# Attention and spectral mixing on one core: turned tokens copied once out of PSUM and split in SBUF, other buffer counts, and a new written order

## The chip, the cores and the metric

The kernel runs on 1 core of one Trainium2 chip. The metric is device time of one execution in microseconds (us). Three executions of the kernel before took 480.16, 479.12 and 478.96 us; their median is 479.12 us. For this kernel a difference of about 0.3% (1.4 us) can be told from none.

## What is computed

```
# attention, per batch (4) and head (8), 768 tokens, head size 64
k_sum = max of k over blocks of 32;  v_sum = mean of v over blocks of 32
scores = [ scale*q@k.T inside a window of 16, scale*q@k_sum.T + log(32) ]
x = softmax(scores) @ [v, v_sum]                 # (4, 768, 512) with heads side by side
# mixing
theta = x @ w_theta
zr, zi = x*cos(theta), x*sin(theta)
y = w_tok_r @ zr + w_tok_i @ zi                  # over the 768 tokens of a batch
u = x + y
out = u + relu(u @ w_ch)
```

Products that need full fp32 accuracy are made of three passes: each operand is split into a high part, rounded to the matrix unit's fp32r, and a low part, the rest; high times high, high times low and low times high are added up in PSUM.

## The kernel before, in words

The four batches have 768 tokens each, which are six tiles of 128 tokens. The page of the profile names engines PE (TensorE), DVE (VectorE), ACT (ScalarE), POOL (GpSimd) and SP (the queue that issues the DMAs).

**Weights.** `w_theta`, `w_tok_r` and `w_tok_i` arrive as 64-bit floats, and `load_f64` (L1341) turns each block into fp32r parts by seven instructions: an absolute value (L1353), a clip (L1357), a shift (L1358), two bitwise joins (L1360, L1362), a cast to the high part (`hi_op`, L1313) and a subtraction for the low part (`lo_op`, L1319). There are four blocks `wth` of 512 columns and twelve blocks `wt` of 768 columns. All of them are made while the first batch is under way. The working tile `f` has two buffers, and the block sums of later batches' values (L1399) load into the same two.

**Per batch.** `prepass` loads the keys (`kn`, two halves of heads) and takes block maxima on DVE (L1382). Three buffers hold `kn`, so one half of the next batch's keys can arrive early. For the first batch the scores read `kn` directly; for later ones POOL or ACT copy the window out of `kn` into a tile `k` with one buffer (L1313, `k<-kn`).

**Per tile of tokens.** `att_tile` makes the scores (L1447); `att_half`, twice, does the masked minimum on DVE (L1460), the exponential on ACT (L1464), the transpose (L1467), a copy `pt`, the product with the values (L1473) and the normalising into `xn` (L1484 or L1486), of which there are two buffers. `turn_tile` (L1490) transposes `xn` into the PSUM bank `t` (L1495), and takes three things out of that bank: `xh` (cast, L1499), `xl` (bank minus `xh`, on DVE, L1500) and `x` (copy, L1501). `theta_tile` (L1513) makes theta in the same bank `t` by twelve matmuls (L1519), and then the angle in `w` (one buffer): L1527 on ACT, L1529 on POOL or DVE, L1530 on DVE, an absolute value (L1535 or L1537) and the two sines (L1541, L1542). Exponential and sine need different tables on ACT, so a change from one to the other costs an ACT_TABLE_LOAD. The two products with `xn` follow (L1550), the first into `w` itself, the second into `zb`; `split_z` makes `zh` and `zl` of each.

**Mixing.** `mix_step` (L1557) adds one tile of 128 tokens into the sums `m` of half the channels. It consists of four groups of six matmuls (L1571), two groups for `wtr` and two for `wti`. A batch has two halves of channels with six steps each. Below, "mixing step 1" is the step with the second tile of the batch.

**End.** After the last attention tile its pools give way to others; `u` goes to memory and back, and `out_unit` (L1602) does the last product (L1618) in eight units, two per batch.

**Order.** Nothing is scheduled automatically. The code above only records operations with what they depend on; the table ORDER (L51 to L1213) says one after another which recorded operation is issued to which engine (V is DVE, A is ACT, G is POOL, P is PE, S is SP), as a step forward or back in the list of operations. Each engine runs its own instructions strictly in that order. Operations such as a cast or a subtraction can stand on either of two engines, and the table decides which.

Of the kernel before, what the change touches and what calls it, by code (L numbers as in the profile page):

```python
# [105 lines left out]
V+12,-11,+1,+183,-125,+124,-123
S+102,-82
A+94,-3
P-159
S+202  # L110
A-42,-118,+111
S-93
P+103,+40
A-202,+172
V-221,+50,+41,+6
A-46,+171,-121
V+154
P-75
A+44,-12
S+85  # L120
A-114,-2
P+32
S-81,+214
A-123,+36,-161
V+4,+1,+151,-150
P+121
V-43,-77,+163,-1
A-53,-108,+120
S+23,+273
P-338  # L130
V+69,-1
P-67,+1
A+72
V-43
A+57
V-3
A+4,-17
V+10,-50
P-29,+40
G+307,-435  # L140
A+158
V-150
A+2,+79
V-71,+72
A+39
V+1
G-111,-8
V+80
A+80,+1
V-41,-111  # L150
P+141
A+1
P+39
V-189,+9
P+154,-43,+31
A-71,+1
V-80,+189,-188
A+121,-2
V-39,+40
G+310  # L160
P-308
G+309
A-430,+191,-110
V+123,-16,-39
P-27,+1,+1
V+65,+12,-11
G-189
V+149,+52
S-192,+16
V+177,-196  # L170
A+4
S+174
A-177
V+72,-68,+70,+69
A+56,-14,-1,-31
V-152,+4
P+149
V+1
A+31,+14,-83,-106
V+145  # L180
G-38
P+69
S-11
P+51
A-39,+10
G-186
S+14
A+171
V-78
A+1  # L190
V+37,-151,+7
A+108
V-114,+7,+217
P-73,+31
V+1
S+36,-1
P-24
A-193
V+114
A+37,+43  # L200
V-11,-68
G-114
V+219,-36,+50,-12,+15
A-84,-37
S-82,+8,+223
A-41,+14
P+76,+1
V-80
P+82
V-165  # L210
P+43
V-188,+189,+25,+172,-157
P-82,+1
G-38
P+39,+1
A-146,-3
V+189
A+28,+2,-1,-28
G-186
V+1  # L220
P+255
A-110
P+70
V-219,+5
G+145
V+110,+1,+2
A-253,+221,+1
S+25,+1
V-107,+111
A-42,+47,-37  # L230
G-219
A+141
P+155
V-295,-6,+7
P+177
A+1,-184,+258,+1
S+115
A-228
V+229
P-149  # L240
S-216,+379,+56
V-178,-82
G-184,+395,-1
V-384
P+292,-1,+3
V-298
P+207
V-67
P+157
V-35  # L250
A-83
V-38
A+79
V+41
A-53,+42,-108,+122
V-1,-54
P-29
V+30
A+177
P-206  # L260
A-180
P+181
G-177
# [1453 lines left out]
```

## Time and profile before

| | |
|---|---|
| median of the runs | 479.12 us (478.96 to 480.16) |
| the profiled execution's own time | 478.45 us |
| its span from first to last instruction | 476.6 us |
| granted TensorE clock over the span | 0.989 |
| busy PE, DVE, ACT, POOL | 446.1, 317.7, 273.7, 101.1 us |
| bytes moved | 62.12 MB, 130 GB/s in the mean |

The rows are read like this. A group's row has line, engine, operation, tile written and tiles read, partitions x elements, the count, and after the bar the busy time, the mean duration of one in ns, and the idle time of the engine just before. A row of a stretch has the stretch in us from the span's start, its length, then the busy time with the number of instructions of PE, of the weight loads (PEld), of DVE, ACT and POOL, then the granted clock, the share of the DMA engines and GB/s. A row of waits has the waiting engine and line, whom it waited for, and total, number and longest in us. A row of the timeline has start, duration, engine, line and operation, and in brackets the idle time before it with what ended it. Tiles and steps are counted here from 0 in each batch.

### The profile page before, as it was taken

The page shows a single profiled execution, that of the slowest core. Times are in us where ns is not written, and L with a number is a line of the kernel's source. Part 1 is how long each engine was busy: PE and PEld are TensorE (multiplying, and loading weights), DVE is VectorE, ACT ScalarE, POOL GpSimd, SP SyncE. Part 2 cuts the span into 40 slices and gives each one's busy share as a digit, 9 for nine tenths or more (in the row PEclk, how much of TensorE's full clock was granted, in tenths as well). Part 3 has the DMA queues.
Part 4 walks back from the last instruction along what each step waited for, and adds up shares of the span by engine and source line. Part 5 has one row for each costly group of instructions (what it writes and reads, how often), then busy time and mean ns, then how long its engine had stood idle before and what let it go on. Part 6 is the DMA issues. An engine that isn't in the chain of part 4 may idle for free.

```text
span 476.6 us, 10041 instructions
## 1 busy us (share of the span) xinstructions
PE 446.1 (94%) x3864; PEld 380.7 (80%) x3864; DVE 317.7 (67%) x905; ACT 273.7 (57%) x582; POOL 101.1 (21%) x124
## 2 busy tenths in 40 slices
PE   0875979999999999999999999999999999999997
PEld 0354867788888888888888888888888889999996
DVE  4989999997574985559556676475655694333343
ACT  2679999878456898956575676656853310001110
POOL 1224244341120021003212110212100413131310
PEclk9988899999999999999999999999999999999999
DMA  8999552065411515024314201110301540724763
GB/s 311 369 342 336 174 191 80 0 233 160 162 57 35 179 65 151 22 77 139 126 52 151 82 30 35 57 41 0 85 1 45 187 145 33 239 99 152 246 209 116
DMA packets 30767, 62.12 MB, mean 130 GB/s; under 512 B 3584, under 2 KB 14080, under 8 KB 30720
## 3 DMA queue, kind: packets, MB, share of 16 engines
q1 hardware_dynamic: 30720, 61.49, 39.2%
q8 instruction: 30, 0.49, 0.4%
q14 instruction: 17, 0.14, 0.1%
HBM read 48.90 MB, written 12.58 MB: 129 GB/s over the span
## 4 chain that ended last, share of the span: by engine, by line
PE 78%; DVE 8%; DMA 6%; issue 3%; ACT 2%; POOL 1%; SPq 0%; ACTq 0%; POOLq 0%; DVEq 0%
PE m L1571 38%; PE c L1618 14%; PE t L1519 12%; PE av L1473 5%; PE p L1467 4%; PE s L1447 3%; DMA wt<-wti 2%; PE t L1495 2%; DMA x<-vn 2%; DMA f<-vT 2%; DVE f L1360 1%; DVE f L1362 1%; DMA kn<-kT 1%; POOL wt L1319 1%; DVE e L1460 1%
## 5 line engine op out<-in xcount | busy, mean ns | idle before, releaser
L1571 PE MATMUL m<-wt,zh 128*128 128x512 f32 (+1 forms) x768 | 170.2, 343 | 0.0
L1571 PEld LDWEIGHTS m<-wt,zh 128*128 128x128 f32 x768 | 119.0, 188 | 16.1 <-issue 0.6
L1571 PE MATMUL m<-wt,zl 128*128 128x512 f32 (+1 forms) x384 | 98.8, 338 | 0.0
L1464 ACT ACTIVATE e<-e,st 128x118 f32<-128x118 f32 x192 | 66.0, 388 | 22.3 <-DVE st L1460 21.5
L1519 PE MATMUL t<-wth,xh 128*128 128x512 f32 x192 | 62.8, 409 | 6.6 <-DVE xl L1500 6.6
L1618 PE MATMUL c<-cuh,wth 128*128 128x384 f32 x256 | 65.6, 337 | 0.0
L1571 PEld LDWEIGHTS m<-wt,zl 128*128 128x128 f32 x384 | 58.7, 188 | 8.5
L1460 DVE CUSTOM_DVE_ANT_0 e<-s,cs 128x118 f32<-128x118 f32 x192 | 46.6, 272 | 8.4 <-PE p L1467 6.2
L1519 PEld LDWEIGHTS t<-wth,xh 128*128 128x128 f32 x192 | 35.0, 194 | 15.1 <-DVE xl L1500 6.0
L1618 PEld LDWEIGHTS c<-cuh,wth 128*128 128x128 f32 x256 | 45.9, 188 | 0.5
L1313 ACT CAST cuh<-cu 128x384 fp32r<-128x384 f32 x20 | 9.6, 511 | 63.9 <-DMA cu<-u_scratch 61.6
L1618 PE MATMUL c<-cul,wth 128*128 128x384 f32 x128 | 43.3, 338 | 0.0
L1623 DVE SCALAR_TENSOR_TENSOR cu<-c,cu 128x384 f32<-128x384 f32 x32 | 17.2, 554 | 39.1 <-PE c L1618 34.9
L1519 PE MATMUL t<-wth,xl 128*128 128x512 f32 x96 | 38.6, 402 | 0.0
L1473 PEld LDWEIGHTS av<-v,pt 118*64 118x64 f32 x768 | 26.8, 138 | 14.6 <-issue 7.7
L1473 PE MATMUL av<-v,pt 118*64 118x65 f32 x768 | 33.3, 229 | 3.0 <-DVE xn L1486 2.6
L1467 PE MATMUL p<-cs,e 128*118 128x128 f32 x192 | 31.1, 285 | 1.6 <-ACT e L1464 0.8
L1529 POOL TENSOR_SCALAR w<-w 128x512 f32<-128x512 f32 x16 | 10.4, 647 | 98.5 <-ACT w L1527 87.5
L1550 DVE TENSOR_TENSOR w<-xn,w 128x512 f32<-128x512 f32 x24 | 17.1, 712 | 18.5 <-ACT w L1542 18.5
L1527 ACT ACTIVATE w<-t,bmagic 128x512 f32<-128x512 f32 x24 | 16.4, 684 | 20.6 <-PE t L1519 14.0
L1319 POOL TENSOR_TENSOR zl<-w,zh 128x512 fp32r<-128x512 f32 x9 | 12.7, 1413 | 72.5 <-DVE zh L1313 39.5
L1319 POOL TENSOR_TENSOR cul<-cu,cuh 128x384 fp32r<-128x384 f32 x17 | 17.0, 1012 | 52.0 <-ACT cuh L1313 32.3
(86 smaller groups left out, 714.5 us busy)
## 6 DMA issues: line engine op xcount, KB each, us to landing
v<-vg SPq DMA_DIRECT2D x48, 195.0 KB, 3.1
q<-qg SPq DMA_DIRECT2D x24, 256.0 KB, 4.9
cu<-u_scratch SPq DMA_DIRECT2D x32, 192.0 KB, 3.2
out<-cu SPq DMA_DIRECT2D x32, 192.0 KB, 2.0
kn<-kT SPq DMA_DIRECT2D x6, 798.0 KB, 7.1
wt<-wtr SPq DMA_DIRECT2D x6, 768.0 KB, 9.4
wt<-wti SPq DMA_DIRECT2D x6, 768.0 KB, 8.7
f<-vT SPq DMA_DIRECT2D x12, 384.0 KB, 4.0
```

Source lines behind the costliest of these rows:

```text
L1319: op(f"VG tt {n}", lambda e: V[e].tensor_tensor(dst(), src(), hi().bitcast(F32), op=ALU.subtract), reads, writes)
L1447: mm("s" if len(parts) == 1 else "s0", [lambda p=p, g=g, h=h, c=c, kk=kk: nc.tensor.matmul(sc[h].get()[ROW[g], p, c], q.get()[ROW[h], p, R ...
L1460: op("V ttr", lambda eng, n=n: nc.vector.tensor_tensor_reduce(e.get()[:, n], sc[n % 2].get()[:, 2 * a + n // 2], mask(m), -SCALE, 3.0e38, ...
L1464: op("A exp", lambda eng, n=n: nc.scalar.activation(e.get()[:, n], e.get()[:, n], AF.Exp, bias=st.get()[:, n:n + 1], scale=-1.0), [(st, n) ...
L1467: mm("tr", [lambda n=n: nc.tensor.transpose(tp.get()[:NK, n], e.get()[:, n], ident()) for n in range(NH)], [e, (cs, "ident")], [tp])
L1473: mm("av", [lambda n=n, g=g: nc.tensor.matmul(xa.get()[ROW[g], n], t.get()[:, n, ROW[g]], v[g].get()[:NK, NH * a + n], start=True, stop=Tr ...
L1519: calls = [lambda t=t, xx=xx, k=k, c=c: nc.tensor.matmul(th.get(), xx.get()[:, c], w_th[c].get()[:, k], start=(c == 0 and t == 0), stop=(c ...
L1527: op(f"A psumb {DM}", lambda e: nc.scalar.activation(r(), th.get(), AF.Identity, bias=bmagic.get(), scale=1.0 / TWO_PI), [th, bmagic], [R])
L1550: op(f"V tt {DM}", lambda e, z=z, hc=hc: nc.vector.tensor_tensor(z(), xn[b, i].get().rearrange("p h d -> p (h d)")[:, None, hc].broadcast_ ...
L1571: nc.tensor.matmul(acc[th], zz.get()[:, r, cc], w_t[s, r].get()[:, k, TT[th]], start=(s == r == t == 0 and (th == 0 or c == 0)), stop=(s = ...
L1618: calls = [lambda t=t, k=k, uu=uu, c=c, co=co, acc=acc: nc.tensor.matmul(acc.get(), w_ch[c].get()[:, k, co * P:(co + 1) * P], uu.get()[:, ...
L1623: op(f"V ttp {HT}", lambda e, co=co, acc=acc: nc.vector.scalar_tensor_tensor(u.get()[:, co], acc.get(), 0.0, u.get()[:, co], ALU.max, ALU. ...
```

## The change

Three things are edited. First, `turn_tile`: the bank `t` is read once, into `x`; `xh` is cast from `x`, and `xl` is `x` minus `xh`, both in SBUF, and the subtraction may now stand on POOL too. Second, buffers: `kn` has two instead of three, `w` two instead of one, `xn` three instead of two. Third, the whole table ORDER is another one. Further code for a variant with split weights is added under `LAG`, which is 0, so it does nothing: the mixing, its weights and its matmuls stay as they were.

```diff
 ORDER = """
-S+64
-A+1
...
+S+80
+V+1,+1,+1,+1,-79,-2
...
-TUNE = dict(XT=1, XB=2, WB=1, TB=1, XNB=2, XHB=2, FB=2, FC=2, QB=2, VB=4, KN=3, ZB=4, ZS=6, EB=2, RING=0, PC=4)
+TUNE = dict(XT=1, XB=2, TB=1, XHB=2, FB=2, FC=2, QB=2, VB=4, ZB=4, EB=2, RING=0, PC=4, WB=2, XNB=3, KN=2, ZS=6, LAG=0, XE=1)
...
-        hi_op(x_h.get, tx.get, DM, [tx], [x_h], psum=True)
-        op(f"V ttp {DM}", lambda e: nc.vector.tensor_tensor(x_l.get(), tx.get(), x_h.get().bitcast(F32), op=ALU.subtract), [tx, x_h], [x_l])
-        hi_op(lambda: x.get()[:, :, i * P:(i + 1) * P], tx.get, DM, [tx], [(x, i)], psum=True)
+        if K["XE"]:
+            here = lambda: x.get()[:, :, i * P:(i + 1) * P]
+            hi_op(here, tx.get, DM, [tx], [(x, i)], psum=True)
+            hi_op(x_h.get, here, DM, [(x, i)], [x_h])
+            lo_op(x_l.get, here, x_h.get, DM, [(x, i), x_h], [x_l])
...
         for r in range(2):
             for c in range(2):
-                mm("m", [lambda r=r, c=c: part(r, c)],
+                    mm("m", [lambda r=r, c=c: part(r, c, (0, 1), z_h, z_l)],
```

The first place is PE in the first batch, around the theta of tile 3 (`t<-wth` is theta, `m<-wt` is mixing; the numbers tell blocks of weights apart). Before, a group of mixing step 1 ends right ahead of that theta:

```order
L1571 MATMUL m_759<-wt_580,zh 128x512
L1571 MATMUL m_760<-wt_580,zh 128x256
L1571 MATMUL m_759<-wt_580,zl 128x512
L1571 MATMUL m_760<-wt_580,zl 128x256
L1519 MATMUL t<-wth_115,xh 128x512 x2
L1519 MATMUL t<-wth_115,xl 128x512
```

In the changed kernel a group of step 0 (`wt_416`) ends there, and the groups of step 1 (`wt_405`) begin behind the theta:

```order
L1626 MATMUL m_858<-wt_416,zl 128x512
L1626 MATMUL m_732<-wt_416,zl 128x256
L1571 MATMUL t<-wth_99,xh 128x512 x2
L1571 MATMUL t<-wth_99,xl 128x512
...
L1571 MATMUL t<-wth_94,xh 128x512 x2
L1571 MATMUL t<-wth_94,xl 128x512
L1626 MATMUL m_858<-wt_405,zh 128x512
L1626 MATMUL m_732<-wt_405,zh 128x256
```

Four groups of mixing (24 matmuls) that stood ahead of this theta now stand behind it.

The second place is DVE around `xl` of tile 5, the last tile of the first batch (`f<-wt` is the making of a block of weights, `e,st<-s` the masked minimum). Before:

```order
L1486 TENSOR_TENSOR xn<-av,st 128x256
L1362 SCALAR_TENSOR_TENSOR f<-wt_753,f 128x768
L1313 CAST wt_1206<-f 128x768
L1313 CAST xh<-t 128x512
L1313 COPY x<-t 128x4x128
L1500 TENSOR_TENSOR xl<-t,xh 128x512
L1399 TENSOR_REDUCE vt<-f 128x24
```

After:

```order
L1506 ISA e,st<-s_1066,cs 128x118
L1506 ISA st 128x1
L1408 SCALAR_TENSOR_TENSOR f<-wt_1001,f 128x768
L1365 TENSOR_TENSOR xl<-x,xh 128x512
L1404 TENSOR_SCALAR f<-f 128x768
L1406 SCALAR_TENSOR_TENSOR f<-wt_297,f 128x768
```

The cast and the copy out of PSUM have left DVE's queue, and the last block of weights (`wt_297`, which was `wt_753`), whose joins stood ahead of this `xl`, now stands behind it.

The third place is SP, where the keys of the second batch are issued (`kn` keys, `wt` weights, `q` queries, `v` values). Before, the first half goes out among the early weights:

```order
L1310 DMA q<-qg 128x512
L1310 DMA v<-vg 96x520
L1310 DMA kn<-kT 128x2x798
L1310 DMA wt_605<-wti 128x1536
L1310 DMA wt_607<-wti 128x1536
L1310 DMA v<-vg 96x520 x2
```

After, both halves go out together, behind the eleventh of the twelve blocks:

```order
L1356 DMA wt_842<-wtr 128x1536
L1356 DMA v<-vg 96x520 x2
L1356 DMA kn<-kT 128x2x798
L1356 DMA q<-qg 128x512
L1356 DMA kn<-kT 128x2x798
L1356 DMA q<-qg 128x512
L1356 DMA v<-vg 96x520 x2
L1356 DMA wt_1001<-wtr 128x1536
```

With two buffers both halves wait until the first batch's last scores (tile 5) have read the buffers; the twelfth block of weights stands behind them in the queue.

More of the change, by code (lines that the diff above doesn't have):

```diff
@@ L106 @@
[L106 to L263, printed above, removed]
@@ L1206 @@
-S+1
-P-15,+1
-V+1
-S+1
-P+3,+1
+S+80
+V+1,+1,+1,+1,-79,-2
+S+53
+A+1
+V+1,+1,+1,+1,+24
+S-21
+A+22
+G+1
+A-22,-3
+S-50,-4
+V+1
+S+13,-16
+V+7,-6
+G+14
+S-11
+V+1
+S+77
+G-22
+P-39
+V+36
+A+26
+S-89,+14
+V+53,+1,+1
+S-68
+V+89
+A-20
+V-41
+A+4
+V+11
+A+4
+P-33
+S+1,-14,+70
+P-55
+S+1
+V+13,-3
+A+4
+S+169
+P-182
+S+4,+81
+V-62
+A-7
+V+10,-2
+G+28
+A+2
+G+1
+S-49
+A+24,-3
+S+50
+V-5,+1,+1,-63
+A+64,-60
+P+2
+A+11
+V+28
+A-55
+V+56,+1,+18
+P+111
+A-169
+G-11
+P+24
+V+55
+S+147,-48
+V+4,+1,-2
+S-5
+A-124,-54
@@ new lines @@
+P+14
+A+1
+S+137,-64
+V+110,-1
+A-170
+V+173,-14
+A+4,-9,+8
+V+10
+A+3,-14,+13
+G-119
+V-66,+1
+G+38
+V+18
+G+1
+V+9
+P-55
+V+1,+1,+1
+P+200
+A-44,+16,+1
+P-44
+V-85,+9
+A+95
+P+12
+V-115
+A+116,-31,+1
+P+31
+V-108,-8
+A+9
+V+77,-76
+P+118
+A-11,-116
+G+1
+V+155,-2
+A-26,-117
+V+144
+P-69
+A+73
+V-42,+40
+S-139
+V-116
+A+256
+V+11
+P-82,+1,+1
+A+84,-55,-99,+141
+V+10,-2,+3
+A-81
+G+1
+P+38
+A+32,+13
+S+74,-49
+P+3
+S-50,-1
+V-139,+1,+1,+1
+A+1,+156,+3
+V-45,+1
+S-97
+V+58
+P+70
+G-142
+V+112
+P+1
@@ new lines @@
+A+224
+S+163
+V-199
+S-175
+A+239,-63
+V+73
+A+4
+V-41,+1,-225,+7
+P+292,-73
+A+42,-41
+P+28
+A+1
+V-255
+A+227
+V-220
+A-6
+V+227
+A-40
+V-47
+P+159
+V-298,+6
+P+260,-12
+A+1
+P+135
+A+52,-432
+V+177
+A+2
+V+78
+P-40
+V+29,+1,+134
+P-163,+1
+G+214
+P-213
+A+1
+G-220,+221
+V-220
+P+283,-27,+29
+V-28
+P+31
+V+107,-15
+A+49,-434,+388,+49
+G-436
+V+385,-123
+A+127,-379
+G+1
+V+214,+38,+123
+A+17
+P-139
+A+1,+125
+V-385,+177
+A+84
+V+132
+A+4
+P-111
+V+109,-3
+A-171
+V-220,+261,-255,+1
+A+388,-13,-381
@@ new lines @@
+V+173
+A+224
+V-390,-6
+A+219
+P+67,-1,+2
+A-280
+V+213,-212
+P+375,-123,+1,+1,+1
+A+1
+S+211,-116
+P+70
+A-207
+P+66
+A+96
+V-119
+S+100,-10
+G-132
+V+208,-165
+A+1,+211
+V-118
+A-92
+V+1
+A+210,-208
+V+85
+P+41
+V+35
+S-79,+4
+G-85
+P+17,+1
+V+154
+G+37
+A-176
+V+141
+P-155,+1
+V+14,+141
+A-136
+V+119
+A+50
+P-187,+1
+V+60
+P-59
+A+139
+V-76
+P+3
+V-64
+P-1
+A+66,+86
+G-82
+A+58
+V+9,+12
+P+37
+A-114,+68,+14
+P-65
+V-62,-24,+4,-2,+85
+A+65,-53,+39
+P-130
+V+115,-35,+1
+P+11
+A+133,-97
+P+3,-130,+1
@@ new lines @@
+A+4
+V-1,-173
+A+47,+44
+G-43
+V+1
+A+1
+P-188,+277
+V+48
+P-321
+V+320,-2
+A-133
+P+76
+V+1
+P-36
+V+1,+1,+35,+1
+P-262
+V+5
+P-8,+2
+A+310,+11
+V-317,+4
+A+438
+S-20
+A+21,-2
+G-217
+P+1
+V-227
+P+228,+1,+1
+G+216
+V-21,-2
+A-192
+G+1
+V+84
+P+118,-88
+A-75
+P+76
+S-344,+291,+1
+A+27,+113
+G+7
+P-170
+V+30,+1
+A+4,+13,-14,+15
+P+126,-138
+A+1
+P+39,-1
+A+93
+P-118,+28
+V-118,-50,+90,-39
+A+1
+V+39,+1
+S-312,+475
+A-253
+P+126
+V+139
+P-174
+V+189
+G-279
+V+277
+A-151
+V+136,+1
+P-96,-3
+A+103,-176,+1
@@ new lines @@
+S+25
+V-29
+P+5
+G-4
+P+16,-216,+224,+1,-8
+V+9,-219
+P+211,+1
+V+1
+P-10,+1,-6,+1
+S+25
+V+1
+A-3
+P-17,-5
+V+23,-22
+S-200,+229,-10
+V+11
+A-3
+S-26
+P+4
+G+26,-6
+V-19
+P-210,+2,+234
+S-25,-245,+251
+V-208,-2
+S+1
+P+229,+17,+1
+V-250,+227
+P+6,+18,-14,+1,+1,+13
+S-251,+260
+V+1
+P-22
+S+15,+3,+6
+V-8
+G+1
+A+2
+G+1,+3
+A+2
+G+1
+P-32,+9
+S-238
+V+230,+18
+P-9
+V-3
+P+4
+S+9
+P-8
+V+1
+P+26
+S-31
+P+37
+S-43
+P+38,+11,-10,+11
+S-38,+43
+P-24,+1,+1,+1,+10
+V+12
+P-11,+1,-6,+11
+V-4,-6
+S+17
+V+1,-24
```

1850 lines of the change are left out of this document (864 added, 986 removed).

## The prediction

> **What bounds the kernel now.** I read the busy line and the slices of the page first.
>
> ```profile
> PE 446.1 (94%) x3864; PEld 380.7 (80%) x3864; DVE 317.7 (67%) x905; ACT 273.7 (57%) x582; POOL 101.1 (21%) x124
> PE   0875979999999999999999999999999999999997
> DVE  4989999997574985559556676475655694333343
> ```
>
> A digit stands for 11.9 us. PE is full from the eleventh slice on; in the first nine it is not, and there DVE is. So I cut the span into stretches at the places where PE starts a theta (columns: PE, weight loads, DVE, ACT, POOL).
>
> ```profile
> 47.30:61.50 14.20, 13.20 (x154) 10.48 (x154) 13.62 (x50) 14.14 (x26) 5.54 (x5) 0.84 0.53 183
> 61.50:75.00 13.50, 12.05 (x134) 9.63 (x134) 13.50 (x29) 13.04 (x29) 6.61 (x8) 1.00 0.55 191
> 75.00:88.20 13.20, 11.33 (x114) 9.05 (x113) 13.06 (x32) 12.99 (x25) 3.60 (x3) 1.00 0.06 16
> 88.20:98.70 10.50, 10.20 (x93) 8.26 (x93) 10.40 (x29) 9.26 (x20) 4.46 (x4) 1.00 0.13 39
> 98.70:108.20 9.50, 9.07 (x77) 7.39 (x77) 8.61 (x26) 6.10 (x11) 3.09 (x6) 1.00 0.83 275
> ```
>
> ```profile
> 120.00:200.00 80.00, 79.77 (x766) 66.99 (x766) 53.25 (x170) 58.33 (x133) 11.66 (x22) 1.00 0.32 100
> ```
>
> From 120 to 200 us PE idles 0.23 us in 80, and its slices stay full behind that: whatever the change does for the other engines there, PE's own work is the same and nothing is to be won. Between 47.3 and 88.2 DVE is busy for 40.18 of 40.9 us and ACT for 40.17, while PE idles 4.3. What PE waits for (stretch 12 to 110 us) is one thing above all:
>
> ```profile
> PE t L1519 <- DVE xl L1500: 6.6, 5, 4.2
> ```
>
> Theta waits for `xl`. Time that PE loses there it never gets back, since it is full afterwards. The time of the kernel is PE's work plus PE's lost time in the first 108 us, and the change can only alter the second, or add losses later. The two last waits for `xl` are those of tiles 4 and 5:
>
> ```profile
> 88.20 0.70 PE L1519 MATMUL t<-wth,xh 128*128 128x512 f32 x2 [0.98 <-DVE xl L1500]
> 98.67 0.70 PE L1519 MATMUL t<-wth,xh 128*128 128x512 f32 x2 [0.17 <-DVE xl L1500]
> ```
>
> **The change, term by term.** The method: count in the two orders what DVE has ahead of these two `xl`, and what PE has ahead of these two thetas. If DVE's part shrinks by more than PE's, PE loses less. The prices:
>
> ```profile
> L1360 DVE SCALAR_TENSOR_TENSOR f<-wt,f 128x768 int32<-128x768 int32 x12 | 13.0, 1087 | 0.1
> L1362 DVE SCALAR_TENSOR_TENSOR f<-wt,f 128x768 uint32<-128x768 uint32 x12 | 12.6, 1049 | 0.0
> L1529 DVE TENSOR_SCALAR w<-w 128x512 f32<-128x512 f32 x8 | 3.9, 486 | 7.1 <-ACT w L1527 7.1
> L1550 DVE TENSOR_TENSOR w<-xn,w 128x512 f32<-128x512 f32 x24 | 17.1, 712 | 18.5 <-ACT w L1542 18.5
> L1313 DVE CAST xh<-t 128x512 fp32r<-128x512 f32 x12 | 8.2, 687 | 3.6 <-PE t L1495 3.6
> L1313 DVE CAST zh<-w 128x512 fp32r<-128x512 f32 x14 | 7.0, 501 | 1.5 <-PE m L1571 1.3
> L1500 DVE TENSOR_TENSOR xl<-t,xh 128x512 fp32r<-128x512 f32 x24 | 16.4, 683 | 2.5 <-ACT xh L1313 2.3
> L1319 DVE TENSOR_TENSOR zl<-zb,zh 128x512 fp32r<-128x512 f32 x14 | 10.7, 766 | 0.1
> L1319 POOL TENSOR_TENSOR zl<-w,zh 128x512 fp32r<-128x512 f32 x9 | 12.7, 1413 | 72.5 <-DVE zh L1313 39.5 <-ACT e L1464 17.4 <-ACT zh L1313 9.3
> L1358 DVE TENSOR_SCALAR f<-f 128x768 int32<-128x768 int32 x12 | 6.7, 562 | 0.0
> L1460 DVE CUSTOM_DVE_ANT_0 e<-s,cs 128x118 f32<-128x118 f32 x192 | 46.6, 272 | 8.4 <-PE p L1467 6.2 <-PE s L1447 1.7 <-issue 0.5
> L1313 DVE COPY pt<-p 118x512 f32<-118x512 f32 x14 | 9.6, 682 | 4.3 <-PE av L1473 3.5 <-PE p L1467 0.8
> L1319 DVE TENSOR_TENSOR wt<-f,wt 128x768 fp32r<-128x768 f32 x5 | 4.8, 957 | 0.0
> ```
>
> An `xl` out of SBUF is not in this trace. Its nearest row is the same subtraction for `zl`, 0.766 us; its ends are the 0.683 of now and the 1.413 of POOL. I take 0.766, since all six of the first batch stand on DVE in the new order. A cast of `x` to `xh` in SBUF is nearest to the cast of `zh`, 0.501.
>
> Tile 4, changed kernel minus before: two bitwise joins fewer (1.087 + 1.049 = 2.14), two L1529 moved to POOL (0.97), one product L1550 later (0.71), three masked minima later (0.82), a shift later (0.56), one copy out of PSUM gone and one cast in SBUF come (0.19): 5.39 us less. Five short ones, on weights and on sums, go three one way and two the other, and I put them at nothing. Five `xl` at 0.083 more each give 0.42 back, so 4.97 us less. PE has four mixing groups fewer ahead of this theta, by the second row here of the chain of waits:
>
> ```profile
> 145.31 0.97 PE s L1447 x32
> ...
> 148.34 1.06 PE m L1571 x6
> ```
>
> That is 4.24 us less to do, so of DVE's 4.97 us only 0.7 reach PE as less loss.
>
> Tile 5: two joins (2.14), two L1529 (0.97), a product (0.71), two shifts or clips (1.12), and three PSUM copies for one SBUF cast (2.06 - 0.50 = 1.56) fewer; one `pt` copy (0.68) and one low part of weights (0.96) more; the short ones again nothing; six `xl` 0.50 more. Together 6.50 - 2.14 = 4.36 us less. PE has one mixing group and one tile of scores less ahead of it, 2.03 us. So 2.3 us reach PE.
>
> Losses add up and never shrink. The first gate alone leaves the lost time 0.7 us lower; the idle time after it (0.30 and 0.43 us in the last two stretches to 108.2) can vanish, so at least 0.7 and about 1.4 us is won by that count, 2.3 by the second. I take the middle of 1.4 and 2.3, **1.9 us**. Ahead of tile 5's `xl` POOL also has two low parts of `wt` fewer than before; what one of those costs DVE is seen below, up to 1.5 us, so a further 0.3 us is put down for the pair, few of which coincide. The sum is 2.2 us.
>
> What I put at nothing: fewer ACT_TABLE_LOADs (36 for 42) and the work that moves between ACT, DVE and POOL after 120 us, because PE's full stretches cover it; if that cover had holes, it would show as idle PE there. The third `xn` and the earlier free bank `t` likewise: PE's transposes waited little for them. The twelfth block of weights is issued behind both key loads, which wait for tile 5's scores; mixing step 5, at the end of the batch, is the only one to use it, and DVE's joins for it stand between the `xl` of tiles 4 and 5. If the load came later than that, DVE and tile 5's `xl` would be held as long as it is late; I put it at nothing.
>
> At the end unit 6 of the last product needs the last mixing step's sums by way of memory (L1587, store, load, split).
>
> ```profile
> 439.53 33.82 PE c L1618 x192
> ```
>
> ```profile
> cu<-u_scratch SPq DMA_DIRECT2D x32, 192.0 KB, 3.2
> ...
> u_scratch<-x SPq DMA_DIRECT2D x16, 256.0 KB, 3.3
> ```
>
> The 192 matmuls are units 4 to 7, 8.5 us each. Before, units 4 and 5 stood between, 16.9 us; in the new order mostly unit 5, 8.5 us, against 6.5 us of DMA with an addition and a split around it. It is just covered, as I count, since unit 6 begins with channels that are there earlier: nothing, at worst 1 us.
>
> The profiled execution took 478.45 us, 0.67 under the median. 478.45 - 2.2 = 476.25, and with the 0.67 the forecast for the median is **476.9 us** (own range 475.4 to 478.2, from gains of 0.9 to 3.7: the lower with `xl` at 1.413 for part of the tiles, the upper with all of POOL's relief).
>
> **A rule against the change.** The new subtraction reads two tiles in SBUF where the old one read one and PSUM. Two pairs of rows, first POOL and then DVE:
>
> ```profile
> 83.54 1.82 POOL L1319 TENSOR_TENSOR wt<-f,wt 128x768 fp32r<-128x768 f32 x1 [0.57 <-ACT wt L1313]
> 96.81 1.85 POOL L1319 TENSOR_TENSOR wt<-f,wt 128x768 fp32r<-128x768 f32 x1 [1.62 <-DVE wt L1313]
> ```
>
> ```profile
> 83.72 2.46 DVE L1360 SCALAR_TENSOR_TENSOR f<-wt,f 128x768 int32<-128x768 int32 x1
> ```
>
> ```profile
> 97.84 0.68 DVE L1500 TENSOR_TENSOR xl<-t,xh 128x512 fp32r<-128x512 f32 x1
> ```
>
> The join with two SBUF operands that started inside POOL's subtraction took 2.46 us against the 1.049 that its twin L1362 takes in the mean, and ended after POOL had; the `xl` out of PSUM that ran inside another took its usual 0.68. So an `xl` out of SBUF can now lose up to 1.5 us to POOL. The Trainium skill, "SBUF — State Buffer", section "Who interferes with whom", says so as a rule: a DVE instruction with two SBUF inputs and a GpSimd instruction that reads SBUF exclude each other, and the second to start waits. These rows agree; by the rule the time is that of the first rival below, without it that of the forecast.
>
> **The rivals.**
> *Nothing is won (25%).* By the mechanism just shown: POOL is busy for 23.3 of the 60.9 us in the first five stretches, so of six `xl` two or three meet it, at 0.8 us in the mean, 2.0 us on DVE, against which the gain of 2.2 is gone. 478.45 - 0.2 + 0.67 = 478.9 us. Against it: much of POOL's time is in instructions of other kinds.
>
> *More is won (17%).* An early hole closes: theta of tile 1 waited longest, and after it the same twelve matmuls were slower.
>
> ```profile
> 47.28 1.22 PE L1519 MATMUL t<-wth,xh 128*128 128x512 f32 x2 [4.18 <-DVE xl L1500]
> ```
>
> ```profile
> 47.28 4.70 PE t L1519 x11
> ...
> 126.30 2.77 PE t L1519 x12
> ```
>
> 4.18 + (4.70 - 2.77) = 6.1 us lie there. With two `w`, tile 1's angle need not wait for tile 0's split, and the engines' queues may flow better: two thirds of it, 4.0 us, on top of 2.2 give 472.9 us. Against it: ahead of tile 1's `xl` DVE's counted work differs by under 1 us.
>
> *Slower (18%).* Two key buffers. Before, a half of the next keys came early; now both wait until the last window has been copied out (batches 2 and 3) or read (batch 1).
>
> ```profile
> kn<-kT SPq DMA_DIRECT2D x6, 798.0 KB, 7.1
> ```
>
> ```profile
> L1382 DVE TENSOR_REDUCE ks<-kn 128x48 f32<-128x1536 f32 x6 | 10.5, 1744 | 0.0
> L1313 POOL COPY k<-kn 128x188 f32<-128x188 f32 x31 | 12.4, 415 | 50.5 <-PE s L1447 22.1 <-ACT e L1464 15.2 <-ACT pt L1313 11.5
> ```
>
> The chain is 0.8 for the two issues, 7.1 for the load, 2 x 1.744 for the maxima, and 0.4 for a copy: 11.8 us. In the new order PE has about 16 us of work between the last scores of one batch and the first of the next (at the change to batch 2 six mixing groups, 6.4 us, two thetas, 5.5, and the short products between them, some 4). It decides at 4.2 us: if the copies, the SP queue or DVE's queue together add more, PE stands still at each of the three changes of batch. At 2 us each, without the gain, 478.45 + 6.0 + 0.67 = 485.1; with it 482.9. I give 482.9.
>
> **How the numbers follow.** Forecast 40%, rivals 25, 17 and 18%. A difference of 0.3%, 1.4 us, is about what a measurement can tell. Faster than 477.7: most of the forecast's range (32 of 40) and the second rival, 49%, and a little of the first, 50%. Slower than 480.5: nearly all of the third rival and a little of the first, 19%. Between, 31%. The range runs from 472.6, past the second rival, to 481.2, which cuts off the greater part of the third.
>
> **What would show it.** Right: in the profile after, PE is full from 120 us on, idle PE between 47 and 108 us falls from 5.05 us (1.00 + 1.45 + 1.87 + 0.30 + 0.43) to about 3, and theta still waits for `xl`. The first rival shows as `xl` rows far above 0.77 us beside POOL. The second as no wait of several us ahead of tile 1's theta. The third as PE waiting at the scores L1493 for copies or keys. Wrong altogether: PE idle in the last 360 us, or `xl` no longer what theta waits for.

## The result and the profile after

The changed kernel takes **475.78 us** (median of 8 runs, 474.62 to 477.18); the kernel before, on the same chips, 480.11 us (8 runs, 478.02 to 480.85). The ratio is 0.9919, with a 95% interval of 0.9897 to 0.9941: 3.9 us less, between 2.8 and 4.9. Forecast were 476.9 us and a gain of 2.2.

The profiled execution of the changed kernel took 476.96 us with a span of 475.2, one of the slower of its eight; that of the kernel before took 478.45, below its median. So the two profiles lie only 1.4 us of span apart. A second profile of the changed kernel, taken later (changed_again, below), has a span of 472.8. Line numbers have moved by about 50: scores L1493, exponential L1510, products with the values L1519, theta L1571, casts L1359, subtractions L1365, mixing L1626.

From the page of the changed kernel, its busy line, PE's slices and the granted clock:

```profile
PE 447.9 (94%) x3864; PEld 382.4 (80%) x3864; DVE 307.6 (65%) x893; ACT 268.9 (57%) x579; POOL 114.3 (24%) x130
PE   0879789998999999999999999999999999999997
PEclk9978899999999999999999999999999999999999
```

PE is full from the eleventh slice on, as before. DVE has 10 us less to do and POOL 13 us more. The stretches between thetas again (same columns as before: PE, weight loads, DVE, ACT, POOL, clock, DMA):

```profile
46.08:61.50 15.42, 12.14 (x206) 9.53 (x206) 14.30 (x51) 14.38 (x31) 4.73 (x4) 0.89 0.50 169
61.50:71.50 10.00, 8.68 (x62) 6.68 (x58) 9.40 (x21) 9.60 (x19) 3.79 (x2) 1.00 0.71 254
71.50:83.15 11.65, 11.41 (x113) 9.10 (x113) 11.48 (x27) 11.49 (x24) 4.75 (x7) 1.00 0.25 86
83.15:95.14 11.99, 11.96 (x83) 10.16 (x79) 11.71 (x35) 11.95 (x25) 4.96 (x5) 1.00 0.08 23
108.00:120.00 12.00, 10.79 (x130) 9.03 (x129) 9.89 (x34) 7.83 (x23) 3.48 (x4) 1.00 0.64 194
120.00:200.00 80.00, 79.92 (x748) 67.61 (x746) 49.34 (x172) 58.76 (x125) 23.19 (x28) 1.00 0.28 90
```

In the two stretches ahead of tile 4's and tile 5's theta (71.5 to 95.1 us) PE idles 0.27 us, where it lost 2.17 before (1.87 + 0.30). But it idles 3.28 ahead of tile 2's theta, before 1.00, and there is a new loss of 1.21 between 108 and 120. PE's longest waits from 12 to 110 us, of which the first is the start, and a short one for `xh`:

```profile
PE s L1493 <- DVE ks L1428: 12.7, 1, 12.7
PE p L1513 <- ACT e L1510: 2.6, 1, 2.6
PE av L1519 <- DVE xn L1532: 1.5, 1, 1.5
PE av L1519 <- ACT xn L1530: 1.1, 1, 1.1
...
PE t L1571 <- DVE xh L1359: 0.3, 1, 0.3
```

The row that led the list before, behind a start of 13.0 us, was theta waiting for `xl` (6.6 us, 5 times); it is gone altogether. In its place stands one wait of 2.63 us, behind theta of tile 1, for exponentials, and a last one at 113.8 us:

```profile
46.08 0.73 PE L1571 MATMUL t<-wth,xh 128*128 128x512 f32 x2 [0.34 <-DVE xh L1359]
52.78 0.65 PE L1513 MATMUL p<-cs,e 128*118 128x128 f32 x4 [2.63 <-ACT e L1510]
113.79 0.69 PE L1519 MATMUL av<-v,pt 118*64 118x65 f32 x16 [1.21 <-DVE xn L1532]
```

What the new splits cost, by groups:

```profile
L1365 POOL TENSOR_TENSOR xl<-x,xh 128x512 fp32r<-128x512 f32 x9 | 12.0, 1332 | 55.2 <-ACT xh L1359 31.6 <-DVE xh L1359 16.7 <-DVE st L1525 6.8
L1365 DVE TENSOR_TENSOR xl<-x,xh 128x512 fp32r<-128x512 f32 x15 | 10.3, 686 | 6.0 <-ACT xh L1359 5.9
L1359 DVE CAST xh<-x 128x512 fp32r<-128x512 f32 x10 | 4.4, 438 | 1.4 <-ACT x L1359 1.3
```

On DVE `xl` takes 0.686 us out of SBUF, about as long as the 0.683 out of PSUM.

### The profile page after: what moved, and what is told of

The parts are those of the page before. It is cut to its first block, busy times and chain, and to the rows that moved or that the text cites. A ratio compares the mean times of both kernels' runs of the same rounds, so it can differ in the third digit from the quotient of the medians.

```text
span 475.2 us, 10024 instructions
## 1 busy us (share of the span) xinstructions
PE 447.9 (94%) x3864; PEld 382.4 (80%) x3864; DVE 307.6 (65%) x893; ACT 268.9 (57%) x579; POOL 114.3 (24%) x130
## 4 chain that ended last, share of the span: by engine, by line
PE 76%; ACT 10%; DMA 6%; issue 3%; DVE 3%; POOL 1%; SPq 1%; ACTq 0%; POOLq 0%; DVEq 0%
PE m L1626 37%; PE c L1686 14%; PE t L1571 11%; PE av L1519 5%; PE p L1513 4%; PE s L1493 3%; DMA q<-qg 2%; PE t L1541 2%; ACT e L1510 2%; DMA x<-vn 2%; DMA kn<-kT 2%; ACT f L1399 1%; ACT wt L1359 1%; ACT L1510 1%; DMA v<-vg 1%
## 5 line engine op out<-in xcount | busy, mean ns | idle before, releaser
L1626 PE MATMUL m<-wt,zh 128*128 128x512 f32 (+1 forms) x768 | 170.1, 343 | 0.0
L1626 PEld LDWEIGHTS m<-wt,zh 128*128 128x128 f32 x768 | 119.1, 188 | 15.9 <-issue 0.3
L1626 PE MATMUL m<-wt,zl 128*128 128x512 f32 (+1 forms) x384 | 98.8, 338 | 0.0
L1510 ACT ACTIVATE e<-e,st 128x118 f32<-128x118 f32 x192 | 66.3, 389 | 12.6 <-DVE st L1506 12.3
L1626 PEld LDWEIGHTS m<-wt,zl 128*128 128x128 f32 x384 | 58.8, 188 | 8.5
L1571 PE MATMUL t<-wth,xh 128*128 128x512 f32 x192 | 62.4, 407 | 0.5 <-DVE xh L1359 0.3
L1506 DVE CUSTOM_DVE_ANT_0 e<-s,cs 128x118 f32<-128x118 f32 x192 | 45.6, 272 | 18.2 <-PE p L1513 11.3
L1359 ACT CAST cuh<-cu 128x384 fp32r<-128x384 f32 x14 | 6.9, 512 | 65.9 <-DMA cu<-u_scratch 53.2
L1519 PEld LDWEIGHTS av<-v,pt 118*64 118x64 f32 x768 | 27.3, 138 | 18.2 <-issue 7.0
L1571 PEld LDWEIGHTS t<-wth,xh 128*128 128x128 f32 x192 | 34.5, 193 | 8.0 <-DVE xh L1359 0.6
L1519 PE MATMUL av<-v,pt 118*64 118x65 f32 x768 | 33.8, 229 | 5.8 <-DVE xn L1532 2.8
L1571 PE MATMUL t<-wth,xl 128*128 128x512 f32 x96 | 38.6, 402 | 0.1
L1365 POOL TENSOR_TENSOR zl<-w,zh 128x512 fp32r<-128x512 f32 x15 | 20.9, 1392 | 62.1 <-DVE zh L1359 34.4
L1365 POOL TENSOR_TENSOR cul<-cu,cuh 128x384 fp32r<-128x384 f32 x15 | 16.0, 1073 | 68.9 <-ACT cuh L1359 33.8
L1359 POOL COPY k<-kn 128x188 f32<-128x188 f32 x34 | 14.2, 429 | 63.2 <-PE s L1493 45.5
L1513 PEld LDWEIGHTS p<-cs,e 128*118 128x118 f32 x192 | 22.1, 141 | 7.4 <-ACT e L1510 3.6
```

Source lines behind the costliest of these rows:

```text
L1359: (nc.scalar.copy if e == "ACT" else V[e].tensor_copy)(dst, src)
L1365: op(f"VG tt {n}", lambda e: V[e].tensor_tensor(dst(), src(), hi().bitcast(F32), op=ALU.subtract), reads, writes)
L1506: op("V ttr", lambda eng, n=n: nc.vector.tensor_tensor_reduce(e.get()[:, n], sc[n % 2].get()[:, 2 * a + n // 2], mask(m), -SCALE, 3.0e38, ...
L1510: op("A exp", lambda eng, n=n: nc.scalar.activation(e.get()[:, n], e.get()[:, n], AF.Exp, bias=st.get()[:, n:n + 1], scale=-1.0), [(st, n) ...
L1513: mm("tr", [lambda n=n: nc.tensor.transpose(tp.get()[:NK, n], e.get()[:, n], ident()) for n in range(NH)], [e, (cs, "ident")], [tp])
L1519: mm("av", [lambda n=n, g=g: nc.tensor.matmul(xa.get()[ROW[g], n], t.get()[:, n, ROW[g]], v[g].get()[:NK, NH * a + n], start=True, stop=Tr ...
```

## The experiments

All ratios are to the kernel before, timed in the same group of runs. Where an edit moves operations, its diff names the operations and not the steps of ORDER. Times from an instruction's start to the end are read from the one profile of a run. The first group:

### new_order_psum_split: new order and buffers, old split

```diff
-TUNE = dict(..., LAG=0, XE=1)
+TUNE = dict(..., LAG=0, XE=0)
 # ORDER: xh, xl, x keep their places; the nine xl of POOL stand at the same places on DVE
```

> The changed kernel with the old turn_tile: xh, xl and x are all taken out of the PSUM bank, and the nine xl that POOL had are on DVE again; order and buffers stay new. Theory O (the gain comes from the new order, the place of the split is worth nothing: a DVE xl takes 0.683 us out of PSUM and 0.686 out of SBUF): 475.5 to 477 us, as the changed kernel (475.8). Rival S (the gain comes from the split in SBUF, which reads the bank once instead of three times and frees it earlier): 479 to 480.5 us, as the kernel before (480.1), with multi-us waits of PE on the bank or on xl.

Measured: 483.76 us, ratio 1.0079 (1.0052 to 1.0106). Slower than both. Its profile has nothing worse in the first 120 us; the loss is in the second batch:

```profile
120.00:200.00 80.00, 74.56 (x649) 62.54 (x648) 46.62 (x155) 51.72 (x111) 14.89 (x21) 0.96 0.26 83
```

```profile
PE t L1572 <- DVE xl L1553: 5.8, 3, 3.8
```

Theory O is refuted as it was put; rival S had the waits right, but not the time (480.5 at most). But the kernel differs in two things: where `xl` reads from, and which engine makes nine of them.

### old_order_sbuf_split: old order and buffers, new split

```diff
-        hi_op(x_h.get, tx.get, ...); op("V ttp", ...); hi_op(x, tx.get, ...)
+        hi_op(x, tx.get, ...); hi_op(x_h.get, x, ...); lo_op(x_l.get, x, x_h.get, ...)
 # ORDER: where xh stood ahead of x, the two take places so that x comes first
```

> The kernel before, order and buffers as they were, with the split in SBUF: x is copied out of the bank first, xh and xl come from x. Theory O: 479.5 to 481 us, as the kernel before, and theta of tile 1 still waits about 4 us. Rival S: 476 to 477.5 us.

Measured: 482.95 us, ratio 1.0032 (1.0006 to 1.0057). By itself the split costs about 1.5 us, a little more than theory O said. Theta of tile 1 still waits, now first for the cast, which comes behind the copy:

```profile
46.38 0.74 PE L1533 MATMUL t<-wth,xh 128*128 128x512 f32 x2 [2.89 <-ACT xh L1321]
47.46 0.50 PE L1533 MATMUL t<-wth,xl 128*128 128x512 f32 x1 [0.34 <-DVE xl L1327]
```

Rival S falls too: the split in SBUF is no gain without the order.

### local_move: the kernel before, tile 1's split ahead of tile 0's sines

```diff
 ACT  w<-w            (L1535, tile 0)
+ACT  x<-t, xh<-t     (tile 1)
 ACT  w<-w, w<-w      (L1541, L1542, tile 0)
-ACT  x<-t, xh<-t     (tile 1)
 DVE  f<-wt           (L1360)
+DVE  xl<-t,xh        (tile 1)
 DVE  f<-wt; e,st<-s; f<-wt; w<-xn,w
-DVE  xl<-t,xh        (tile 1)
```

> The kernel before, with three operations moved at one place: the copies x and xh of tile 1 stand on ACT ahead of the sines of tile 0 instead of behind them, and xl of tile 1 stands on DVE three joins earlier. It closes the hole of 4.18 us ahead of theta of tile 1 by some 2.5 us. Theory H (time that PE gets there is kept to the end): 476.5 to 478 us, the idle time of PE from 47 to 108 us as before. Rival P (from 47 to 88 us DVE is full and sets the pace, so that the next thetas come when DVE's xl come, not earlier): 479.5 to 480.5 us, with PE's later waits longer by what the hole lost.

Measured: 482.22 us, ratio 1.0031 (1.0011 to 1.0051): about 1.5 us slower, which neither theory said. The hole shrank from 4.18 to 1.35 us, and a wait of 4.82 came right behind it:

```profile
46.21 0.73 PE L1519 MATMUL t<-wth,xh 128*128 128x512 f32 x2 [1.35 <-DVE xl L1500]
54.08 1.13 PE L1473 MATMUL av<-v,pt 118*64 118x65 f32 x16 [4.82 <-ACT pt L1313]
...
92.49 0.71 PE L1519 MATMUL t<-wth,xh 128*128 128x512 f32 x2 [0.99 <-DVE xl L1500]
```

The wait of 4.82 us is for `pt`, which ACT makes behind the two sines, two table loads and exponentials, in the same order as before. It ends 17.3 us behind the first theta (54.03 - 36.69); in the kernel before it was 17.0 (51.98 - 34.94). So ACT sets the pace here, and PE waits at the next place instead. Theory H's gain did not come; but as the wait only moved, this run does not show what time really won there would be worth. In this profile theta of tile 4 starts 4.3 us later than in the one of the kernel before, of which 1.75 are there at the first theta already, ahead of the edit. From theta of tile 4 to the end it is 388.4 us in both (480.9 - 92.49, 476.6 - 88.20): behind it nothing of the move is left.

### hole_back: the changed kernel, tile 0's sines ahead of tile 1's copy

```diff
+ACT  w<-w            (L1587, tile 0)
+ACT  w<-w, w<-w      (L1593, L1594, tile 0)
 ACT  x<-t            (tile 1)
-ACT  w<-w            (L1587, tile 0)
 ...
-ACT  w<-w, w<-w      (L1593, L1594, tile 0)
```

> The changed kernel with one place undone: on ACT the absolute value and the two sines of tile 0 stand ahead of tile 1's copy x again. Tile 1's theta then comes some 3 us later. Theory H: 478 to 479 us. Rival P: 475.3 to 476.8 us, as the changed kernel, since the wait of 2.63 us for the exponentials behind theta of tile 1 shrinks by as much, and DVE sets the pace after that.

Measured: 477.06 us, ratio 0.9919 (0.9888 to 0.9950), the ratio of the changed kernel. The hole is back:

```profile
34.80 0.73 PE L1571 MATMUL t<-wth,xh 128*128 128x512 f32 x2
...
47.42 1.22 PE L1571 MATMUL t<-wth,xh 128*128 128x512 f32 x2 [2.75 <-DVE xh L1359]
```

The wait of 2.63 us for the exponentials went in exchange, and by the medians the closed hole is not what the change won. A part of up to some 2 us stays inside the interval, and the profiles point to one: from the first theta to the end it is 440.6 us here (475.4 - 34.80), against 438.6 and 439.3 in the two profiles of the changed kernel.

The second group of runs asked what the nine subtractions do, and which waits count.

### sbuf_xl_on_dve: the changed kernel, POOL's nine xl on DVE

```diff
-POOL xl<-x,xh        (tiles 2 to 5 of the second batch, five of later batches)
+DVE  xl<-x,xh        (the same nine, at the same places of the order)
```

> The changed kernel, split in SBUF, with its nine POOL subtractions xl put on DVE at the same place of the order; nothing else. Theory Q (the 5.3 us that the split out of PSUM lost in the new order, at the thetas at 158.8 and 189.3 us, are those of a subtraction that stands in DVE's queue behind products that wait for ACT's sines, wherever it reads from): 481 to 484 us, with the same two waits of PE of about 1.5 and 3.8 us for xl. Rival T (they are those of the PSUM bank, read three times): 475 to 477 us, no such waits.

Measured: 481.82 us, ratio 1.0048 (1.0023 to 1.0074). The same two waits are there, 0.98 and 3.20 us (1.54 and 3.75 in new_order_psum_split):

```profile
159.52 0.51 PE L1572 MATMUL t<-wth,xl 128*128 128x512 f32 x1 [0.98 <-DVE xl L1366]
189.66 0.50 PE L1572 MATMUL t<-wth,xl 128*128 128x512 f32 x1 [3.20 <-DVE xl L1366]
```

DVE's rows ahead of the second show why. `xh` was ready at 183.9 us (a cast on ACT from 183.27, 0.61 long), but a product ahead in DVE's queue waits 1.80 us for ACT's sine, and other work follows:

```profile
187.25 0.69 DVE L1606 TENSOR_TENSOR w<-xn,w 128x512 f32<-128x512 f32 x1 [1.80 <-ACT w L1595]
...
188.12 0.69 DVE L1360 COPY pt<-p 118x512 f32<-118x512 f32 x1
...
188.92 0.69 DVE L1366 TENSOR_TENSOR xl<-x,xh 128x512 fp32r<-128x512 f32 x1
```

In the changed kernel POOL made this one, and theta did not wait:

```profile
184.75 1.29 POOL L1365 TENSOR_TENSOR xl<-x,xh 128x512 fp32r<-128x512 f32 x1 [1.59 <-ACT xh L1359]
```

Theory Q holds: it is the queue, not the bank. Of the 6.2 to 7.5 us that the ratios show to the changed kernel these waits are 4.2; the clock behind them (0.98 over 80 us) makes up some 1.6. The rest is not traced.

### first_batch_psum: split out of PSUM in the first batch alone

```diff
-        if K["XE"]:
+        if b:
```

> The changed kernel with the split out of PSUM in the first batch alone, where all six subtractions xl stand on DVE in either form; the later batches split in SBUF. Theory L (in SBUF the three steps are a chain, x, then xh, then xl, longer by one copy of 0.6 us ahead of each theta, while out of PSUM x is no part of it): 472 to 474.5 us, 2 to 3 us faster than the changed kernel. Rival O (the place of the split is worth nothing where POOL has no part in it): 475 to 477 us.

Measured: 474.71 us, ratio 0.9904 (0.9877 to 0.9931). Against 0.9919 and 0.9891 of the changed kernel that is no difference. Where POOL has no part in it, the place of the split is worth nothing that these times can tell; the 2 to 3 us of theory L do not show. A smaller gain stays open: from the first theta (34.53) to the end its profile has 437.1 us, against 438.6 and 439.3.

### joins_ahead: the changed kernel, last block's joins ahead of tile 5's xl

```diff
 DVE  f<-wt           (L1408, the block before)
+DVE  f<-f, f<-wt, f<-wt   (L1404, L1406, L1408, the last block)
 DVE  xl<-x,xh        (tile 5)
-DVE  f<-f, f<-wt, f<-wt
```

> The changed kernel with one part undone that the prediction counted: the shift and the two joins of the last block of weights (0.56 + 0.96 + 0.95 = 2.47 us) stand on DVE ahead of tile 5's xl again. The xl of tile 5 ended at 93.7 us and its theta began at 95.1, so 1.4 us are hidden. Theory G (the thetas of tiles 4 and 5 are the gates): theta of tile 5 comes some 1.0 us later and PE waits for xl there; 476.3 to 477.5 us. Rival W (another wait sets the end, the one for xn at 113.8 us): 475.3 to 476.3 us.

Measured: 475.08 us, ratio 0.9910 (0.9890 to 0.9929): no change, and a little below what rival W said. PE waits 0.37 us at tile 5's theta:

```profile
94.60 0.50 PE L1571 MATMUL t<-wth,xl 128*128 128x512 f32 x1 [0.37 <-DVE xl L1365]
```

From this theta's start (93.53) to the end it is 380.8 us, in the two profiles of the changed kernel 380.1 and 380.0. So of the 2.47 us at least 1.7 were hidden.

### first_batch_psum_late_v: a copy moved behind the last wait

```diff
-DVE  v<-vs           (ahead of st and xn)
 DVE  st<-st, xn<-av,st
+DVE  v<-vs
```

> The kernel of first_batch_psum with one more operation moved: on DVE a copy of the next batch's summed values (up to 1.65 us) stands behind the normalising into xn instead of ahead of it. PE waits 1.2 us for that xn in the changed kernel, its last wait of any size. If such a wait counts in full: 1.2 us less than first_batch_psum, 471 to 473.3 us. If it is only covered up by another: the same as first_batch_psum.

Measured: 473.32 us, ratio 0.9874 (0.9853 to 0.9895). The wait of 1.2 us is gone, and the median is 1.4 us below that of first_batch_psum. The intervals of the two overlap, but size and sign are the expected ones, and the profiles agree: from tile 5's theta to the end it is 378.5 us (471.5 - 92.98), in first_batch_psum 379.8 (471.6 - 91.82). With exps_first, below, it is the fastest of the study.

The third group:

### changed_again: the changed kernel beside them

> The changed kernel itself, timed beside the others of this group so that they can be set against it: 475 to 477 us, a ratio to the kernel before of 0.990 to 0.994. If the chain x, xh, xl of the split in SBUF costs what theory L said, it lies 2 us or more above first_batch_psum in its ratio (above 0.994); if the place of the split is worth nothing, at the same ratio (0.9904) within 0.003.

Measured: 474.98 us, ratio 0.9891 (0.9863 to 0.9919). This also gives the second profile.

### tile4_late: 2.7 us of DVE's work ahead of tile 4's xl

```diff
+DVE  zb<-xn,w; wt<-f,wt; f<-wt   (L1605, L1365, L1408)
 DVE  xl<-x,xh        (tile 4)
-DVE  zb<-xn,w; wt<-f,wt; f<-wt
```

> The changed kernel with 2.7 us of DVE's work put ahead of tile 4's xl: a product, a low part of weights and a join, which stand right behind it now. Its theta, which came 0.3 us after the xl, then comes 2.2 to 2.5 us later. Theory G (time that PE loses at this theta is not made up later): 477.5 to 478.5 us. Rival W (something else sets the end, and PE only waits here instead of there): 475 to 476.5 us.

Measured: 477.34 us, ratio 0.9928 (0.9905 to 0.9951), against changed_again 2.4 us more by the medians, 1.8 by the ratios. The intervals overlap, and the changed kernel's first ratio, 0.9919, is close. The profile is clearer. PE started the first two matmuls of theta and waited 1.41 us at the third:

```profile
82.14 0.73 PE L1568 MATMUL t<-wth,xh 128*128 128x512 f32 x2
...
84.28 0.50 PE L1568 MATMUL t<-wth,xl 128*128 128x512 f32 x1 [1.41 <-DVE xl L1362]
```

From 82.14 us to the end it is 393.5 us, in the two profiles of the changed kernel 392.1 (475.2 - 83.15) and 391.9 (472.8 - 80.87): 1.4 to 1.5 more, the length of the wait. The time is just short of what theory G expected, and outside what W did. In this profile the time lost at tile 4's theta is not made up.

### exps_first: the wait for exponentials made shorter

```diff
 ACT  e<-e,st         (first of the four)
-ACT  e<-e,st (other half); zh<-w (tile 0)
 ACT  e<-e,st x3
+ACT  e<-e,st (other half); zh<-w (tile 0)
```

> The kernel of first_batch_psum_late_v with two operations moved on ACT: the last exponential of the other half and the cast zh of tile 0 stand behind the three exponentials that PE waits for at 51.8 us, so that this wait of 1.94 us shrinks by 0.8. Theory H (time won there is kept): 472 to 472.8 us. Rival P (from 47 to 88 us DVE and ACT are full and set the pace, as the closed hole showed): 473 to 473.8 us, as without the move.

Measured: 473.82 us, ratio 0.9858 (0.9826 to 0.9889); without the move 473.32 and 0.9874. No gain that shows. The wait shrank from 1.94 to 1.02 us, and the next one appeared 3 us behind it:

```profile
51.64 0.65 PE L1513 MATMUL p<-cs,e 128*118 128x128 f32 x4 [1.02 <-ACT e L1510]
...
55.10 0.62 PE L1513 MATMUL p<-cs,e 128*118 128x128 f32 x4 [1.53 <-DVE st L1525]
```

### joins_behind: the kernel before, DVE relieved ahead of both gates

```diff
-DVE  f<-f, f<-wt     (shift and the join of 2.46 us, ahead of tile 4's xl)
 DVE  xl<-t,xh        (tile 4)
+DVE  f<-f, f<-wt
 ...
-DVE  f<-wt; wt<-f    (join and cast, ahead of tile 5's xl)
 DVE  xl<-t,xh        (tile 5)
+DVE  f<-wt; wt<-f
```

> The kernel before, with DVE's part of the count alone: a shift and the join of 2.46 us stand behind tile 4's xl instead of ahead of it, and a join with its cast behind tile 5's. PE's order is untouched. Theory G: the waits of 0.98 and 0.17 us at these two thetas go, 1 us less than the kernel before (a ratio of 0.997 to 0.998), and no more, since PE itself is late then. Rival W: the same time as before (0.999 to 1.002).

Measured: 483.50 us, ratio 1.0065 (1.0038 to 1.0092), slower, which neither theory said. The two waits at the thetas are gone, but the thetas come no earlier in this profile (89.20 and 100.28 us, before 88.20 and 98.67). Behind them are new waits, from the work that was put off:

```profile
104.45 0.97 PE L1566 MATMUL m<-wt,zh 128*128 128x512 f32 x4 [0.68 <-ACT zh L1308]
109.50 0.95 PE L1442 MATMUL s<-k,q 64*64 64x118 f32 x20 [0.47 <-DVE st L1455]
...
112.15 0.50 PE L1396 MATMUL av<-cs,vt 128*24 128x128 f32 x3 [0.71 <-DVE vt L1394]
```

From tile 5's theta (100.28 us) to the end it is 381.4 us, where the kernel before has 377.9: what was put off in DVE's queue is missed further on. The rest of PE's order needs those results.

## Why the forecast came out, step by step

**By its own signs.** The time came out inside the range, but only in part for the reasons given. Of the three signs of being right one came, PE full from 120 us on. Idle PE from 47 to 108 us did not fall to about 3 us (4.74, below). And theta no longer waits for `xl`, which was named as a sign of being wrong altogether: PE's waits moved to other places. So that the time came near is in part luck.

**The bound.** That only PE's lost time in the first 108 us can move held, apart from the wait at 113.8: from 120 to 440 us PE idles 0.13 us. But that this leaves the work after 120 us without weight was wrong. "The work that moves between ACT, DVE and POOL after 120 us" was put at nothing "because PE's full stretches cover it". The cover is thin: with the nine subtractions on DVE in the same places, the whole gain and 0.5% more are gone. The new order stands on POOL's share, which came with the split in SBUF; in the kernel before this subtraction is written for DVE alone. That edit was priced at tile 4 as an exchange of 0.19 us and 0.42 for five slower `xl`, and POOL's share after 120 us at nothing.

**The counts at the two gates.** In operations they were right, in time too small. The `xl` of tile 4, before and after, and that of tile 5 after:

```profile
87.37 0.68 DVE L1500 TENSOR_TENSOR xl<-t,xh 128x512 fp32r<-128x512 f32 x1
```

```profile
82.19 0.68 DVE L1365 TENSOR_TENSOR xl<-x,xh 128x512 fp32r<-128x512 f32 x1
```

```profile
93.04 0.68 DVE L1365 TENSOR_TENSOR xl<-x,xh 128x512 fp32r<-128x512 f32 x1
```

They start 5.18 us (87.37 to 82.19) and 4.80 us (97.84 to 93.04) earlier; counted were 4.97 and 4.36. That looks like a hit, but in changed_again it is 7.46 and 7.09 (79.91 and 90.75). DVE's busy time from the start to these `xl` says more: 77.94 us before and 70.30 after, 7.6 less, and 88.31 and 80.91, 7.4 less (70.45 and 81.05 in changed_again). Most of what the count missed, some 3 us, are two joins. Before, they ran inside subtractions of POOL and took 2.46 us (shown in the prediction) and 1.89, where the others take about 0.95:

```profile
61.37 1.89 DVE L1362 SCALAR_TENSOR_TENSOR f<-wt,f 128x768 uint32<-128x768 uint32 x1
```

In the new order the longest such join ahead of these `xl` takes 1.15 us. The prediction had the joins at their mean and 0.3 us for POOL's relief; on DVE the two meetings had cost 2.4. Tile 5's theta has 2.1 us more of span behind it than before (475.2 - 95.14 = 380.06 against 377.93), about the 2.03 us of work that was counted as moved behind it.

**What they are worth.** Here the step "losses add up and never shrink" failed. It is so from tile 4's theta on: 1.41 us lost there cost about as much (tile4_late), 1.2 us saved at 113.8 gave about as much (first_batch_psum_late_v). It is not so ahead of that: a wait closed or opened at tile 1's theta, or behind it, did not move the end by a matching amount (hole_back, exps_first, local_move). Ahead of tile 4's theta DVE and ACT are nearly full in both kernels (before 40.2 and 40.2 of 40.9 us, after, from 46.1 to 83.2, 35.2 and 35.5 of 37.1), and PE only chooses where it waits. So idle PE from 47 to 108 us, forecast to fall by 2 us, fell by 0.6 (61.00 - 55.66 = 5.34 before, 61.00 - 56.26 = 4.74 after) while the time fell by 3.9; it was the wrong measure. And of DVE's joins of the last block, 2.1 us of the count for tile 5, most could be put back unseen. No run puts back the whole count at tile 4 or PE's four mixing groups, so how much of the gain the two gates made is not shown.

**The size.** The sum of 2.2 us was too small: 3.9 (2.8 to 4.9) was measured, and 5.2 (3.9 to 6.6) the second time. The first theta of the three profiles, before, changed, and changed_again, and tile 5's theta of the last:

```profile
34.94 0.73 PE L1519 MATMUL t<-wth,xh 128*128 128x512 f32 x2 [0.68 <-DVE xl L1500]
```

```profile
36.56 1.20 PE L1571 MATMUL t<-wth,xh 128*128 128x512 f32 x2
```

```profile
33.46 0.73 PE L1571 MATMUL t<-wth,xh 128*128 128x512 f32 x2
...
92.83 0.70 PE L1571 MATMUL t<-wth,xh 128*128 128x512 f32 x2
```

From the first theta to the end it is 441.7 us before, and 438.6 and 439.3 in the changed kernel: 3.0 and 2.3 us less, near the 2.2 that was worked out for this part. What lies ahead of the first theta had no term in the sum, and something is won there. PE's first scores, before and after:

```profile
13.02 0.42 PE L1447 MATMUL s<-ks,q 64*64 64x24 f32 x8 [13.02 <-DMA q<-qg]
```

```profile
12.75 0.43 PE L1493 MATMUL s<-ks,q 64*64 64x24 f32 x8 [12.75 <-DVE ks L1428]
```

Before, they wait for the first load of queries, which SP issues at 5.32 us; the new order issues it at 3.15, and they wait for the maxima of the keys instead. In the four profiles with the old order they start at 13.02 to 14.05 us, in the ten with the new one at 12.03 to 12.75, in the mean 1.3 us earlier. At the first theta the ranges overlap: it starts at 34.94, 36.61 and 36.69 us with the old order and split, at 33.46 to 36.56 (mean 34.7) in six profiles with the new ones. So part of the gain beyond the 2.2 seems to lie at the start; no run moved this load alone.

**The rivals.** *Nothing is won*: no `xl` came near 1.4 us on DVE, the mean is 0.686. Of the six of the first batch one met POOL at all, and POOL's instruction began 0.2 us behind it (46.20 and 46.41). On other operations the cost is there: a `zl` with two SBUF inputs that began at 104.77 inside POOL's own `zl` (104.13 to 105.42) took 1.20 us, against a mean of 0.763, and a product `zb` that began at 263.57 inside one of POOL's `xl` (263.25 to 264.54) took 1.53, against some 0.69. In twelve of the thirteen such meetings that the timeline of this profile shows singly the delay is what POOL's instruction had left, less 0.13 to 0.14 us. From 120 us on they cost PE nothing that shows (0.13 us idle up to 440). The Trainium skill's rule ("SBUF — State Buffer", section "Who interferes with whom") is that the second to start waits. These rows agree.

*More is won*: the hole closed as this rival said (4.18 to 0.34 us), and the time came out between it and the forecast, but by hole_back's median the one is not the cause of the other. The twelve matmuls behind the hole, which the rival called slower, ran at a granted clock of 0.50:

```profile
48.00:50.00 2.00, 2.00 (x6) 1.53 (x5) 2.00 (x11) 1.99 (x5) 0.80 (x1) 0.50 0.28 102
```

*Slower by two key buffers*: behind the wait at 113.8 us PE idles 0.13 us up to 440, so no batch change waits for keys; the last product has no wait either. What other buffer counts would do to either order was not tried.

## What to carry to other kernels

In this kernel a wait was worth its length only where the waiting engine is full from there to the end; upstream of that, while other engines set the pace, closing it only moved it. An operation that can stand on a third engine is worth more than its price says if the queue that it leaves is in order and waits for others: count what stands ahead of it, not only its duration. A relief by putting work off has to be followed to the place where that work is due.

## What the hardware showed

The granted clock differs between executions of one kernel, and by enough to matter. The changed kernel's two profiles, same columns as above, first the one with a span of 475.2 us and then the one with 472.8:

```profile
24.00:30.00 6.00, 3.27 (x92) 2.62 (x86) 4.15 (x24) 4.45 (x14) 3.27 (x4) 0.95 1.03 300
30.00:39.00 9.00, 8.27 (x98) 7.04 (x94) 7.34 (x25) 5.67 (x12) 1.65 (x2) 0.50 1.03 343
```

```profile
24.00:30.00 6.00, 4.27 (x148) 3.63 (x150) 4.64 (x24) 5.13 (x14) 3.66 (x4) 1.00 1.04 319
30.00:39.00 9.00, 6.75 (x94) 4.92 (x88) 8.93 (x29) 8.26 (x21) 2.29 (x2) 1.00 1.04 349
```

In this stretch one ran at half clock for 9 us, the other not at all. Over the eight runs of the changed kernel the four with a mean clock of 0.986 took 476.32 to 477.18 us, the four at 0.992 to 0.996 took 474.62 to 475.25. The Trainium skill, "TensorE: Matmul & The Clock Gate", section "What's actually happening", gives a reason why runs differ: the activity window is free-running and does not start with the kernel. The traces fit such a window: ahead of 60 us the stretches at half clock last 3.4 and 6.8 us in the kernel before, 10.2 and 3.4 us in the first profile of the changed kernel and 3.4 us in the second, whole multiples of about 3.4. The Trainium skill says in the same section that the clock falls after an idle window of about 3.4 us. Here it fell at 29.4 us; in the 3.4 us ahead of that PE was busy for 1.34 us, and its longest single wait was 1.55, so no wait of that length was needed.
